# Linear attention and a two-layer network: decays kept over units of 256 tokens, another division of the weights' decoding, 48-column weight loads, new figures in the scheduler

## The chip, the cores and the metric

The kernel runs on one core of one Trainium2 chip. The metric is the time of one execution on the device in microseconds (us). Engines are called by their names in the profile too: TensorE (PE, and PEld for its weight loads), VectorE (DVE), ScalarE (ACT), GpSimd (POOL), and SP, whose queue issues most DMAs.

## The reference

A gated linear attention over 4 batches, 8 heads, 768 tokens and 48 dimensions a head feeds a network of 384, 2048 and 384 columns, all in fp32:

```python
for t in range(S):
    kt, vt, rt, wt = (k[:, :, t], v[:, :, t], r[:, :, t], w[:, :, t])
    cur = np.einsum('bhd,bhe->bhde', u[None] * kt, vt)
    y[:, :, t] = np.einsum('bhd,bhde->bhe', rt, state + cur)
    state = wt[:, :, :, None] * state + np.einsum('bhd,bhe->bhde', kt, vt)
...
h = x @ w_in                       # x: attention's output, (B * S, 384)
g = np.where(pos, h, np.where(neg, 0.0, (h + beta) ** 2 / (4.0 * beta)))
return (g @ w_out).astype(np.float32)
```

`w` is drawn evenly from 0.8 to 0.95, `r`, `k`, `v` and `u` are normal with a spread of 0.1.

## The kernel before

**Units and chunks.** Attention works in 12 units of 256 tokens (UT), three to a batch, and each unit in four chunks of 64 (C, NC). All eight heads of a unit are held at once as four pairs on two tiles (`q`), each head in 64 partitions (HP) of which 48 (D) carry data.

**Attention of one unit** (`attention`, from L350 on). Two scans on VectorE (L405 forward, L400 backward, both in `scan`) give for each chunk the running product P of the decays and its inverse; the seeds tile restarts the running product in every chunk, and `ptot` keeps each chunk's last P (L425). L428 makes k/P and L478 makes r P, in place. `among` (L448) multiplies both in 64x64 tiles, all against all tokens of a chunk; L454 (`picked`) keeps what lies below the diagonal. In the first four units (EARLY) the diagonal with u is made in the same way from k times u, which `with_u` (L416, GpSimd) computes with one instruction for each half of a tile, with u as a per-partition scalar; later units make it from L466, L468, L471 and L474. `ktrans` (L487) transposes k/P on TensorE, ScalarE copies it (L494), `umat` (L509) multiplies it with v, and `chain` (L525 to L528, VectorE) carries the state from chunk to chunk: add, then multiply by the chunk's P. `cross` and `along` (both L550, through `put` and `inter`) add the states' part and the part within a chunk to y. L602 to L606 split y into a rounded part and a rest for the network; six DMAs a unit (L649, `fill`) spread the fourth pair of heads into the rows that the others leave free.

**The network** (`products`, from L694 on). Blocks of 512 tokens (two units) go through 16 slices of 128 hidden columns. Each slice takes nine matmuls in (L896, `product_in`: high times high, low times high, high times low, for three slices of rows) and nine out (L916, `product_out`), two slices later (LAG). Between them, the gate: L712 and L713 on ScalarE, L714 on VectorE, L716 rounds on ScalarE, L717 gives the rest on VectorE. HALVES splits some slices into two halves of 256 tokens, one unit each: the first 5 of block 0 and the first 11 of block 1. So block 0 can begin with unit 0 alone.

**Weights** (`weight`, from L309 on). They come as 64-bit words. For each of the 16 slices: load (L317), magnitude of the high word (L326, ScalarE), low bits (L329, ScalarE) and sign (L330, GpSimd) into the two halves of one buffer `rr`, both joined with the magnitude (L332, VectorE), the high part rounded (L322, ScalarE), and the low part as a difference (L335, VectorE). There is one `rr`, two `fl`, and three loads may be in flight.

**Order of the work.** Nothing is left to run-time choice. `Plan` records every operation with an engine, a cost in us and what it reads and writes; `port=True` marks those that use the port which VectorE and GpSimd share, and they are never planned at the same time. `order` plays them through with those costs, HOP us from one engine to the next, and picks on each engine the ready one that is due first; `best` repeats this six times (ROUNDS) and keeps the order that ends first. LEADS, DECODE, SLACK, STEP, FIRST and PACED set the dues at the start. `kept_warm` puts matmuls on zeros (L304) into planned gaps of TensorE; `warm` (L298) does the same at the start. The emitted order then holds on each engine, in sequence.

**Guard.** `check` looks at the end whether all P are at least P_MIN and all decays at most 1; if not, `general` computes everything again.

## Time and profile before

| what | value |
|---|---|
| median of 3 runs | 529.23 us (528.53 to 530.14) |
| span of the profiled execution | 526.9 us |
| TensorE busy | 503.0 us (95%), 5438 matmuls |
| its weight loads (PEld) | 412.2 us (78%) |
| VectorE busy | 340.4 us (65%), 592 instructions |
| ScalarE busy | 294.4 us (56%), 596 instructions |
| GpSimd busy | 108.8 us (21%), 76 instructions |
| mean granted clock of TensorE | 0.991 |
| moved by DMA | 54.22 MB |

The span runs from the first to the last instruction of one execution; the runs' times contain a little more around it. In the profile's rows, "xN" is the number of instructions, "busy, mean ns" their time together and the mean of one, and behind the second bar stands the idle time of the engine just ahead of them with what ended most of it. A timeline's row has the start, the length, engine, line, operation, and the idle time before it in brackets. A row of the chain has the start, the length and what it was. Matmuls overlap, so a busy TensorE isn't TensorE at its peak; the step from one group's start to the next group's start is the better measure.

### The profile page before, as it was taken

How to read it: one execution, taken by the hardware profiler on the slowest of the kernel's cores; microseconds unless marked ns; L12 is line 12 of the kernel's file. 1: busy time of each engine (PE TensorE's matmuls, PEld its weight loads, DVE VectorE, ACT ScalarE, POOL GpSimd, SP SyncE). 2: the span in 40 equal slices, each digit the busy share in tenths (PEclk: the TensorE clock that was granted, in tenths of full speed). 3: DMA queues.
4: the chain of work that ended last, by engine and by line, in shares of the span. 5: the costliest groups of instructions: out<-in, count | busy, mean ns of one | idle time of the engine just before them, and what ended most of it. 6: DMA issues, size and time to landing. Idle time of an engine off the chain costs nothing.

```text
span 526.9 us, 12832 instructions
## 1 busy us (share of the span) xinstructions
PE 503.0 (95%) x5438; PEld 412.2 (78%) x5438; DVE 340.4 (65%) x592; ACT 294.4 (56%) x596; POOL 108.8 (21%) x76
## 2 busy tenths in 40 slices
PE   7778899999999999999999999999999999999993
PEld 5557787788999988887877778887787777788882
DVE  5989799999897868324398869445833545333331
ACT  1387698878786556433464736443744444444441
POOL 6496865740203021000111011101000100000000
PEclk9899999999999999999999999999999999999997
DMA  8865472344835171100234404103200100100001
GB/s 321 344 240 179 152 318 81 122 148 145 271 104 181 44 237 48 61 0 3 82 125 140 151 20 151 56 2 109 78 0 2 41 17 12 66 0 1 0 0 67
DMA packets 21921, 54.22 MB, mean 103 GB/s; under 512 B 3104, under 2 KB 8672, under 8 KB 21856
## 3 DMA queue, kind: packets, MB, share of 16 engines
q1 hardware_dynamic: 21568, 52.93, 29.2%
q8 instruction: 44, 0.72, 0.5%
q10 hardware_dynamic: 288, 0.39, 0.2%
q14 instruction: 21, 0.17, 0.1%
HBM read 46.43 MB, written 4.72 MB: 97 GB/s over the span
## 4 chain that ended last, share of the span: by engine, by line
PE 77%; POOL 6%; DVE 5%; issue 4%; DMA 3%; ACT 1%; SPq 1%; ACTq 0%; DVEq 0%; POOLq 0%
PE h L896 35%; PE acc L916 33%; POOL rr L330 4%; PE bank L550 3%; POOL nk L416 3%; PE bank L509 2%; PE bank L448 2%; PE bank L487 1%; DMA rk<-in_rk 1%; DVE fl L332 1%; SPq L649 1%; DMA cst<-in_consts 1%; DVE y L400 1%; DVE p L405 1%; DVE gl L717 1%
## 5 line engine op out<-in xcount | busy, mean ns | idle before, releaser
L896 PE MATMUL h<-x,wt 128*128 128x512 f32 (+1 forms) x1008 | 223.7, 367 | 2.4 <-DVE wt L335 1.5
L896 PEld LDWEIGHTS h<-x,wt 128*128 128x128 f32 x1008 | 169.6, 188 | 36.2 <-DVE wt L335 2.2
L916 PE MATMUL acc<-gh,wt 128*128 128x512 f32 (+1 forms) x672 | 156.4, 368 | 0.0
L714 DVE SCALAR_TENSOR_TENSOR g<-g,h 128x512 f32<-128x512 f32 (+1 forms) x112 | 67.9, 606 | 99.8 <-ACT g L713 97.5
L916 PEld LDWEIGHTS acc<-gh,wt 128*128 128x128 f32 x672 | 114.0, 188 | 22.1 <-issue 0.5
L712 ACT ACTIVATE g<-h 128x512 f32<-128x512 f32 (+1 forms) x112 | 60.0, 536 | 116.6 <-PE h L896 113.4
L717 DVE TENSOR_TENSOR gl<-g,gh 128x512 fp32r<-128x512 f32 (+1 forms) x112 | 71.5, 640 | 35.6 <-ACT gh L716 35.6
L916 PE MATMUL acc<-gl,wt 128*128 128x512 f32 (+1 forms) x336 | 86.1, 364 | 1.1 <-DVE gl L717 1.1
L716 ACT CAST gh<-g 128x512 fp32r<-128x512 f32 (+1 forms) x112 | 62.2, 556 | 44.4 <-DVE g L714 42.1
L916 PEld LDWEIGHTS acc<-gl,wt 128*128 128x128 f32 x336 | 58.7, 188 | 12.5 <-DVE gl L717 1.5
L713 ACT ACTIVATE g<-g 128x512 f32<-128x512 f32 (+1 forms) x112 | 63.9, 571 | 3.2
L474 POOL TENSOR_TENSOR r<-cst,d 128x512 f32<-128x512 f32 x16 | 16.8, 1070 | 227.5 <-PE bank L550 207.9
L330 POOL TENSOR_SCALAR rr<-wraw 128x768 uint16<-128x768 f32 x16 | 51.6, 3227 | 28.4 <-DVE fl L332 25.1
L405 DVE TENSOR_TENSOR_SCAN p<-wq,seeds 128x520 f32<-128x520 f32 x24 | 30.8, 1283 | 3.1 <-DMA wq<-in_w 2.3
L400 DVE TENSOR_TENSOR_SCAN y<-wq,seeds 128x520 f32<-128x520 f32 x24 | 30.4, 1266 | 0.8
L466 POOL TENSOR_TENSOR nk<-nk 128x768 f32<-128x768 f32 x8 | 15.3, 1914 | 52.5 <-DMA nk<-in_nk 52.5
L416 POOL TENSOR_SCALAR nk<-rk,cst 128x256 f32<-128x256 f32 x16 | 22.5, 1417 | 3.4 <-DMA cst<-in_consts 2.6
L428 DVE TENSOR_TENSOR rk<-rk,y 128x512 f32<-128x512 f32 x24 | 17.9, 745 | 3.6 <-POOL nk L416 2.3
L329 ACT ACTIVATE rr<-wraw 128x768 uint16<-128x768 uint32 x16 | 17.4, 1085 | 1.1 <-DMA wraw<-in_wbits 1.1
L550 PEld LDWEIGHTS bank<-rk,st 64*64 64x64 f32 x656 | 12.3, 134 | 6.9 <-issue 3.7
L454 DVE COPY_PREDICATED r<-below,bank 128x512 f32<-128x512 int32 x22 | 15.1, 727 | 4.0 <-PE bank L448 4.0
L478 DVE TENSOR_TENSOR rk<-rk,p 128x512 f32<-128x512 f32 x24 | 17.4, 736 | 0.3 <-PE acc L448 0.3
(104 smaller groups left out, 398.7 us busy)
## 6 DMA issues: line engine op xcount, KB each, us to landing
rk<-in_rk SPq DMA_DIRECT2D x24, 512.0 KB, 4.6
wraw<-in_wbits SPq DMA_DIRECT2D x16, 768.0 KB, 7.1
wq<-in_w SPq DMA_DIRECT2D x24, 260.5 KB, 2.8
nk<-in_nk SPq DMA_DIRECT2D x8, 768.0 KB, 4.6
vn<-in_v SPq DMA_DIRECT2D x11, 384.0 KB, 6.7
fl<-in_w SPq DMA_DIRECT2D x12, 260.0 KB, 3.1
out_y<-g SPq DMA_DIRECT2D x10, 256.0 KB, 2.5
x<-last SPq DMA_DIRECT2D x66, 32.0 KB, 2.9
```

What stands on the lines that cost most here:

```text
L330: op("POOL", 2.0, due, [("raw", f)], ["rr_high"], lambda: G.tensor_scalar(out=r16[:, :, 1], in0=wraw[f][:, :, 1].bitcast(F32), scalar1=0.0 ...
L400: V.tensor_tensor_scan(out=y_[:, ::-1], data0=w[:, SEG:0:-1], data1=sv[:, ::-1], initial=0.0, op0=ALU.mult, op1=ALU.add)
L405: V.tensor_tensor_scan(out=pv[:, q].rearrange("p n c -> p (n c)"), data0=w[:, 0:SEG], data1=sv, initial=0.0, op0=ALU.mult, op1=ALU.add,)
L416: G.tensor_scalar(out=ku[:, q, cs], in0=rk[slot[q]][:, 1, cs], scalar1=u_col[:, 2 * q + pr : 2 * q + pr + 1], scalar2=None, op0=ALU.mult)
L550: PE.matmul(out=bank[by[g]][HP * half : HP * half + HP, lo : lo + C], start=first, stop=False, skip_group_check=True, **kw)
L712: op("ACT", c, due, [("b", 6 + hk)], [("g", gk)], lambda: nc.scalar.activation(gs, hs, AF.Relu, scale=0.5, bias=0.5))
L713: op("ACT", c, due, (), [("g", gk)], lambda: nc.scalar.activation(gs, gs, AF.Square))
L714: op("DVE", 0.13 + 0.53 * k, due, [("b", 6 + hk)], [("g", gk)], lambda: nc.vector.scalar_tensor_tensor(out=gs, in0=gs, scalar=1.0, in1=hs, ...
L716: op("ACT", c, due, [("g", gk)], [("gh", gk)], lambda: nc.scalar.copy(ghs, gs))
L717: op("DVE", 0.15 + 0.5 * k, due, [("g", gk), ("gh", gk)], [("gl", gk)], lambda: nc.vector.tensor_tensor(out=gls, in0=gs, in1=ghs.bitcast(F ...
L896: nc.tensor.matmul(hp, lhsT=wx[f][:, cs], rhs=xt[:, j, :], start=n == 0, stop=n == 8)
L916: nc.tensor.matmul(o[j], lhsT=wx[f][:, cs], rhs=gt, start=first and i == 0, stop=stop and i == 2, skip_group_check=True)
```

## The change

- The running product is kept over the whole unit of 256 tokens instead of each chunk of 64. P_MIN goes from 2^-58 to 2^-64; seeds, `ptot` and the layout of w follow. `chain` now only adds in each chunk; one multiplication by the unit's P (`carry`) at the end of a unit makes the next unit's first state.
- The sign of the weights is masked out with one instruction on VectorE into `rr`, ScalarE then writes the low bits into the lower halves, and the low part (the difference) moves to GpSimd, not marked with `port`.
- k times u is one tensor product a tile on GpSimd, with u broadcast, in place of two instructions with a scalar.
- The weight loads of `umat` take 48 columns of k instead of 64, those of `cross` and `along` 48 columns of state or v (64 still in units 0 and 6, INPLACE), and the states' part contracts over 48 rows instead of 64.
- `warm` writes zeros of 512 columns to all eight banks, in place of eight matmuls of 128 columns to one.
- The scheduler gets new costs, a shorter HOP, a latency with which an engine's next operation may begin before the last one's end, a price for turning between 64x64 tiles and the full array, separate leads for each weight (DECODES), and new dues.

The diff, cut to its core:

```diff
-SEG = 2 * NC * (C + 1)
+SEG = 2 * (UT + 1)
-P_MIN = 2.0**-58
+P_MIN = 2.0**-64
...
-    HOP = 0.15
+    HOP = 0.04
+    LATENCY = {"PE": 0.16, "DVE": 0.083, "ACT": 0.1}
+    TURN = {64: 0.33, 128: 0.10}
+    ISSUE = 0.75
...
-            free[e] = end[n] = t + op["cost"]
+            end[n] = t + op["cost"]
+            if e == "PE" and op["mode"] != mode:
+                mode = op["mode"]
+                end[n] += self.TURN[mode]
+            free[e] = end[n] - late.get(e, 0.0)
...
-SLACK = 1.95
-LEAD, DECODE = 15, 4.5
-STEP, FIRST, PACED = 4.9, 24.0, 4.6
+SLACK = 5.214
+LEAD = 15
+STEP, FIRST, PACED, AFTER = 10.1576, -2.570, 9.5357, 4.9
...
     def warm():
-        for _ in range(WARM):
-            PE.matmul(hp[0][:, 0:128], lhsT=zero, rhs=zero, start=True, stop=True)
+        for b in bank:
+            PE.matmul(b, lhsT=zero, rhs=zero.unsqueeze(1).broadcast_to([128, 4, 128]), start=True, stop=True)
...
-        op("ACT", 1.07, due, [("raw", f), ("flight", f % FLIGHT)], ["rr_low"],
+        op("DVE", 0.5, due, [("raw", f)], ["rr"], lambda: V.tensor_scalar(
+            out=rr, in0=wraw[f][:, :, 1], scalar1=-(2**31), scalar2=None, op0=ALU.bitwise_and))
+        op("ACT", 1.07, due, [("raw", f), ("flight", f % FLIGHT)], ["rr"],
            lambda: A.activation(r16[:, :, 0], wraw[f][:, :, 0].bitcast(U32), AF.Copy, scale=LOW))
-        op("POOL", 2.0, due, [("raw", f)], ["rr_high"], lambda: G.tensor_scalar(
-            out=r16[:, :, 1], in0=wraw[f][:, :, 1].bitcast(F32), scalar1=0.0, scalar2=32768.0, op0=ALU.is_lt, op1=ALU.mult))
-        op("DVE", 0.95, due, ["rr_low", "rr_high"], [("fl", k)], lambda: V.scalar_tensor_tensor(
+        op("DVE", 0.95, due, ["rr"], [("fl", k)], lambda: V.scalar_tensor_tensor(
             out=m, in0=m, scalar=3, in1=rr, op0=ALU.logical_shift_left, op1=ALU.bitwise_or), port=True)
         op("ACT", 0.83, due, [("fl", k)], [("wh", f), ("raw", f)], split)
-        op("DVE", 0.95, due, [("fl", k), ("wh", f)], [("wl", f)], lambda: V.tensor_tensor(
-            out=w_lo[f], in0=s, in1=w_hi[f].bitcast(F32), op=ALU.subtract), port=True)
+        op("POOL", 1.8, due, [("fl", k), ("wh", f)], [("wl", f)], lambda: G.tensor_tensor(
+            out=w_lo[f], in0=s, in1=w_hi[f].bitcast(F32), op=ALU.subtract))
-        plan.group(first, when, DECODE)
+        plan.group(first, when, DECODES[f])
...
         def with_u(q):
-            for pr in range(2):
-                cs = slice(pr * UT, pr * UT + UT)
-                G.tensor_scalar(
-                    out=ku[:, q, cs], in0=rk[slot[q]][:, 1, cs], scalar1=u_col[:, 2 * q + pr : 2 * q + pr + 1],
-                    scalar2=None, op0=ALU.mult)
+            G.tensor_tensor(
+                out=ku[:, q].rearrange("p (n c) -> p n c", c=UT), in0=parts(q, 1),
+                in1=u_col[:, 2 * q : 2 * q + 2].unsqueeze(2).broadcast_to([128, 2, UT]), op=ALU.mult)
...
-                            i, o = slice(HP * g, HP * g + HP), slice(HP * h, HP * h + HP)
+                            i, o = slice(HP * g, HP * g + HP), slice(HP * h, HP * h + D)
...
-            if old is None:
-                V.tensor_tensor(out=out, in0=up, in1=pt, op=ALU.mult)
-                return
-            V.tensor_tensor(out=sm, in0=up, in1=ss_(old), op=ALU.add)
-            V.tensor_tensor(out=out, in0=sm, in1=pt, op=ALU.mult)
+            if old is None:
+                V.tensor_copy(ss_(new), up(c))
+            else:
+                V.tensor_tensor(out=ss_(new), in0=up(c), in1=ss_(old), op=ALU.add)
+        def carry(new):
+            V.tensor_tensor(out=ss_(new), in0=sm, in1=ptot[:, 4 * u : 4 * u + 4].unsqueeze(2).broadcast_to([128, 4, D]), op=ALU.mult)
...
+        wide = HP if u in INPLACE else D
-            PE.matmul(out=bank[by[g]][HP * half : HP * half + HP, lo : lo + C], start=first, stop=False, skip_group_check=True, **kw)
+            PE.matmul(out=bank[by[g]][HP * half : HP * half + wide, lo : lo + C], start=first, stop=False, skip_group_check=True, **kw)
...
-            i = slice(HP * h, HP * h + HP)
-            put(g, pair, h, c2, lhsT=wide_st[s][i, pair * HP : pair * HP + HP] if s in wide_st else st[s][i, pair * D : pair * D + HP],
+            i = slice(HP * h, HP * h + D)
+            put(g, pair, h, c2, lhsT=wide_st[s][i, pair * HP : pair * HP + wide] if s in wide_st else st[s][i, pair * D : pair * D + wide],
...
-                                put(g, pair, h, c2, lhsT=vs(i, c2, 2 * pair + h, HP), rhs=r_[h][i, pair, c2, :])
+                                put(g, pair, h, c2, lhsT=vs(i, c2, 2 * pair + h, wide), rhs=r_[h][i, pair, c2, :])
```

More of the change, by code (lines that the diff above doesn't have):

```diff
@@ L73, in add @@
         self.ops.append(dict(e=engine, cost=cost, emit=emit, due=due, deps=deps, port=port, size=size,
-                             fresh=fresh and engine == "PE", touch={*reads, *writes}))
+                             fresh=fresh and engine == "PE", touch={*reads, *writes}, mode=mode))
         return n
@@ L127, in order @@
                 users[m].append(n)
-        free, end, begin, lands = {}, {}, {}, []
+        free, end, begin, lands = {"SP": self.ISSUE}, {}, {}, []
         port = bus = 0.0
-        open_ = {}
+        mode = 128
+        late = self.LATENCY
+        open_ = {e: [] for e in ("PE", "SP", "ACT", "DVE", "POOL")}
         since = {}
@@ L135, in opened @@
             op = ops[n]
-            since[n] = max((end[m] + (0.0 if ops[m]["e"] == op["e"] and not ops[m]["size"] else self.HOP) for m in op["deps"]), default=0.0)
-            open_.setdefault(op["e"], []).append(n)
+            since[n] = max((end[m] + (-late.get(op["e"], 0.0) if ops[m]["e"] == op["e"] and not ops[m]["size"] else self.HOP)
+                            for m in op["deps"]), default=0.0)
+            open_[op["e"]].append(n)
         def ready(n):
@@ L240, in attention_moe @@
     minus_one = one([128, 1], F32, "minus_one")
-    seeds = one([128, 2 * NC, C + 1], F32, "seeds")
+    seeds = one([128, 2, UT + 1], F32, "seeds")
     zero = one([128, 128], F32, "zero")
     look = one([1, 2], F32, "look")
-    ptot = one([128, 16 * NU], F32, "ptot")
+    ptot = one([128, 4 * NU], F32, "ptot")
     above = one([128, 2 * NU], F32, "above")
@@ L296, in warm @@
     def warm():
[L297 to L300 removed]
+        for b in bank:
+            PE.matmul(b, lhsT=zero, rhs=zero.unsqueeze(1).broadcast_to([128, 4, 128]), start=True, stop=True)
+    op("PE", 5.5, SOON, ["zero"], [("b", i) for i in range(8)], warm)
     def zeros(b, us):
@@ L524, in chain @@
             if old is None:
-                V.tensor_tensor(out=out, in0=up, in1=pt, op=ALU.mult)
-                return
-            V.tensor_tensor(out=sm, in0=up, in1=ss_(old), op=ALU.add)
-            V.tensor_tensor(out=out, in0=sm, in1=pt, op=ALU.mult)
-        for c in range(NC - (third == UB - 1)):
-            old, new = before[-1], (state["st"] + 1) % STATES
-            if alone and c < NC - 1:
+                V.tensor_copy(ss_(new), up(c))
+            else:
+                V.tensor_tensor(out=ss_(new), in0=up(c), in1=ss_(old), op=ALU.add)
@@ L533, in attention @@
+        def carry(new):
+            V.tensor_tensor(out=ss_(new), in0=sm, in1=ptot[:, 4 * u : 4 * u + 4].unsqueeze(2).broadcast_to([128, 4, D]), op=ALU.mult)
+        for c in range(NC - 1):
+            old = before[-1]
+            if alone:
                 new = list(wide_st)[c]
             else:
-                state["st"] = new
-            op("DVE", 0.35 if old is None else 0.71, due, [("b", bu[c % 2]), ("ptot", u, 0), ("ptot", u, 1)] + ([("s", old)] if old is not None else []),
-               [("s", new), "sm"], lambda c=c, old=old, new=new: chain(c, old, new), port=True)
+                new = state["st"] = (state["st"] + 1) % STATES
+            op("DVE", 0.36, due, [("b", bu[c % 2])] + ([("s", old)] if old is not None else []), [("s", new)],
+               lambda c=c, old=old, new=new: chain(c, old, new), port=True)
@@ L538, in attention @@
             before.append(new)
+        if third != UB - 1:
+            old = before[-1]
+            new = state["st"] = (state["st"] + 1) % STATES
+            op("DVE", 0.36, due, [("b", bu[1]), ("s", old)], ["sm"], lambda old=old: V.tensor_tensor(
+                out=sm, in0=up(NC - 1), in1=ss_(old), op=ALU.add), port=True)
+            op("DVE", 0.36, due, ["sm", ("ptot", u, 0), ("ptot", u, 1)], [("s", new)], lambda new=new: carry(new), port=True)
         by = [take(), take()]
         begun = set()
+        wide = HP if u in INPLACE else D
```

78 lines of the change are left out of this document (38 added, 40 removed).

## The prediction, made before the change was run

> **What bounds the kernel now.** I read the table of windows first, with the edges put where TensorE's pattern changes. After each stretch's length stand the busy times of PE, PEld, DVE, ACT and POOL, then the granted clock.
>
> ```profile
> 0.00:28.90 28.90, 22.23 (x362) 15.77 (x363) 21.16 (x34) 10.16 (x21) 17.40 (x29) 0.94 0.90 334
> 28.90:62.70 33.80, 26.49 (x519) 22.79 (x517) 28.66 (x51) 23.93 (x47) 27.30 (x14) 1.00 0.53 195
> 62.70:518.50 455.80, 454.24 (x4559) 373.64 (x4559) 290.18 (x510) 259.63 (x529) 64.14 (x35) 1.00 0.25 81
> ```
>
> From 62.70 to 518.50 TensorE is busy for 454.24 of 455.80 us. No other engine can shorten that stretch: only less TensorE work, or more of it done before 62.70, does. The 8.4 us from there to the end of the span, 526.9, are copies and stores that the change leaves alone. So the next view is the chain that ended last, which steps from group to group there and so gives what each costs from one start to the next.
>
> ```profile
> 72.14 2.10 PE h L896 x9
> 74.24 1.09 PE bank L448 x64
> 75.33 2.31 PE h L896 x9
> ...
> 84.83 1.08 PE bank L509 x64
> ...
> 92.43 0.63 PE bank L550 x32
> 93.05 2.31 PE h L896 x9
> 95.36 1.56 PE bank L550 x96
> ```
>
> Nine products of 512 columns cost 2.10 us, and 0.2 more behind a group of 64x64 tiles. In the tiled groups, L550's 96 instructions less its 32 take 0.93 us: 16 rounds of four (one to each quarter of the array) at 58 ns. L509 streams 48 columns and L448 streams 64, yet 64 instructions take 1.08 and 1.09 us: the streamed columns don't set the round. What did TensorE achieve before 62.70? Its groups in that window say:
>
> ```profile
> L896 PE MATMUL h<-x,wt 128*128 128x256 f32 x72 | 11.0, 292 | 1.6 <-DVE wt L335 1.5
> ```
>
> 72 first products of 256 columns are eight groups of nine at half of 2.1 us, and the second products trail by up to two steps (LAG), so six groups: some 14 x 1.05 = 14.7 us. Attention for units 0 and 1, with 2 x 1.09 for L448, 1.08 for L509, 0.63 + 1.56 for L550 and about 1 for transposes (two at 0.4 to 0.6 by the plan's costs in the diff), is 6.5 us each, with one more L448 group 14 together, and the turns of mode 2. So about 31 us of 62.7 were useful and 32 were idle, filler or slow. This is the second place where time can come from.
>
> Why so late? The first half of block 0 runs only five weights (HALVES); then unit 1 must be ready. The timelines of VectorE, GpSimd, the SP queue and TensorE show its path:
>
> ```profile
> 11.59 0.69 DVE L428 TENSOR_TENSOR rk<-rk,y 128x512 f32<-128x512 f32 x1 [0.76 <-POOL nk L416]
> ...
> 49.05 0.48 DVE L604 TENSOR_TENSOR last<-bank,last 128x128 fp32r<-128x128 f32 x2
> ```
>
> ```profile
> 6.14 5.41 POOL L416 TENSOR_SCALAR nk<-rk,cst 128x256 f32<-128x256 f32 x4 [2.56 <-DMA cst<-in_consts]
> ```
>
> ```profile
> 22.92 0.81 SPq L277 DMA_DIRECT2D rk<-in_rk  x2
> ...
> 49.59 3.94 SPq L649 DMA_DIRECT2D x<-last  x6
> ```
>
> ```profile
> 56.75 2.30 PE L896 MATMUL h<-x,wt 128*128 128x256 f32 x18
> ```
>
> Unit 1's r and k (L277) load only at 22.92, when unit 0 gives the buffer back, and land 4.6 us later:
>
> ```profile
> rk<-in_rk SPq DMA_DIRECT2D x24, 512.0 KB, 4.6
> ```
>
> So at about 27.5; its last VectorE step ends at 49.53, 22 us on. In the window 28.90 to 62.70 VectorE was busy 28.66 of 33.80 us, GpSimd 27.30: decoding weights and unit 1 fight for them. Six fills take 3.94 us of the queue, and unit 1's first products start at 56.75.
>
> **The change, part by part.** *Weights.* Rows of GpSimd's and VectorE's groups:
>
> ```profile
> L330 POOL TENSOR_SCALAR rr<-wraw 128x768 uint16<-128x768 f32 x16 | 51.6, 3227 | 28.4 <-DVE fl L332 25.1 <-DMA wraw<-in_wbits 3.4
> L416 POOL TENSOR_SCALAR nk<-rk,cst 128x256 f32<-128x256 f32 x16 | 22.5, 1417 | 3.4 <-DMA cst<-in_consts 2.6 <-PE bank L448 0.9
> L474 POOL TENSOR_TENSOR r<-cst,d 128x512 f32<-128x512 f32 x16 | 16.8, 1070 | 227.5 <-PE bank L550 207.9 <-DVE g L714 19.6
> L466 POOL TENSOR_TENSOR nk<-nk 128x768 f32<-128x768 f32 x8 | 15.3, 1914 | 52.5 <-DMA nk<-in_nk 52.5
> ```
>
> ```profile
> L332 DVE SCALAR_TENSOR_TENSOR fl<-fl,rr 128x768 int32<-128x768 int32 x16 | 15.5, 971 | 3.2 <-POOL rr L330 3.1
> L335 DVE TENSOR_TENSOR wt<-fl,wt 128x768 fp32r<-128x768 f32 x16 | 15.2, 949 | 1.0 <-ACT wt L322 1.0
> ...
> L528 DVE TENSOR_TENSOR st<-sm,ptot 128x192 f32<-128x192 f32 x38 | 13.9, 366 | 1.4
> ...
> L673 DVE TENSOR_SCALAR ptot<-ptot 128x192 f32<-128x192 f32 x1 | 0.3, 259 | 0.0
> ```
>
> GpSimd loses 3.23 us a weight and gets the subtraction, like L466: 1.91. The ring through the single rr buffer was 3.23 + 0.97 us; it becomes mask, the low bits on ScalarE, and the OR: 0.6 + 1.1 + 0.97, some 2.7 (1.1 is the plan's cost of L329, which stays as it is). VectorE loses 0.95 and gets the mask. No row shows that instruction. L673, the same operation, did 192 elements in 259 ns, where L528's two tensors needed 366: half the cycles per element, so 768 would take about 0.56 (an estimate); a full-rate one like L335 takes 0.95. I take 0.56: 0.39 less a weight, nothing at the other end. The OR (L332) now waits on ScalarE's low bits behind a mask of its own engine; what stands behind it on VectorE, unit 1's multiplies and the gates L714 and L717, waits along. A wait of the whole 1.1 us would cost more than the mask saves.
>
> *k times u.* Two L416 of 1.42 become one tensor product like L474, 1.07, so four at the start drop from 5.41 to 2.1 us. VectorE's L428 waited 0.76 for them in the row at 11.59, and there are two such multiplies a unit. Taken: 1.5 us at unit 0, and about 1.7 a unit for GpSimd after.
>
> *Decay over whole units.* The chain loses its L528 per chunk but for one: two operations fewer in a batch's first unit, three in the others. At 0.37 that is 0.7 to 1.1 us a unit off VectorE. The scans keep their lengths within 6 of 520 elements. The wide seeds and the smaller ptot save nothing that counts. If the new limit of 2^-64 were broken, the general path would run; with decays drawn evenly from 0.8 to 0.95, 256 of them multiply to about 2^-50, with a spread near one bit, so I leave it out.
>
> *Start of unit 1, summed.* Unit 0 ends 2 us sooner (1.5 + 0.7, some of it lost to longer warm-up fills), so the load lands at 25.5. The 22 us after it hold four L335 (-3.8) and four masks (+2.2), three chain steps (-1.1), and some of the 5.1 us in which VectorE idled in that window, of which I count 2 as gone: 22 becomes 17.5, give or take 3. The last VectorE step ends near 43 instead of 49.5, and the products start near 50 instead of 56.75. TensorE's wait for a decoded weight (1.5 us in L896's row above) goes too. That is 8 to 9 us less idle; I take 9. Cover: if VectorE is late again, ScalarE and GpSimd are not the next limit in that window (23.93 and 27.30 of 33.80 busy, GpSimd to be relieved). The fills' 6 us stay.
>
> *48-column loads.* Load rows:
>
> ```profile
> L896 PEld LDWEIGHTS h<-x,wt 128*128 128x128 f32 x1008 | 169.6, 188 | 36.2 <-DVE wt L335 2.2 <-DMA x<-last 1.3 <-issue 0.5
> ...
> L550 PEld LDWEIGHTS bank<-rk,st 64*64 64x64 f32 x656 | 12.3, 134 | 6.9 <-issue 3.7 <-DVE g L714 1.1 <-ACT gh L716 0.7
> L550 PEld LDWEIGHTS bank<-r,vn 64*64 64x64 f32 x704 | 11.8, 134 | 0.0
> L509 PEld LDWEIGHTS bank<-vn,kt 64*64 64x64 f32 x704 | 11.3, 134 | 4.1 <-issue 1.8 <-ACT kt L494 0.9 <-ACT gh L716 0.4
> ```
>
> 64 columns more cost 188 - 134 = 54 ns, 0.84 a column, nearly a whole round of 58. If loads set the round, 16 columns fewer save 13.5 ns of it. Rounds concerned: L509 in all 12 units, 12 x 16 = 192; L550 in the ten units outside INPLACE, (656 + 704 - 112)/4 = 312 (unit 6 keeps its 112). 504 x 13.5 = 6.8 us, all but some 0.2 in the stretch where TensorE is the end of the chain. If instead a fixed cost per instruction sets the round, the gain is 0. I take 6.8, because equal times for 48 and 64 streamed columns point at the load.
>
> The Trainium skill, "TensorE: Matmul & The Clock Gate", section "LDWEIGHTS (loading the stationary operand)", gives a load time of columns over 1.2 GHz; an estimate by it is 13.3 ns a round, 6.7 us, which agrees with the rows. "TensorEngine Tiling (Array Packing)", section "Instruction Overhead", speaks against: about 60 cycles for each matmul, so that narrow ones cost the same; by it the term could be 0.
>
> *Scheduler.* It only reorders. In the packed stretch there are 1.56 us of idle to win or lose; smaller assumed hops (0.04 instead of 0.15) leave less slack in each fixed order. I take 0, with 2 either way.
>
> Sum: 526.9 - 6.8 - 9 = 511.1 us of span. The median of the runs, 529.23, stands 2.3 above the profiled span, so 513.4, rounded to **513**. Its own range is 508 to 518.
>
> **Rivals.** *A, the start is not won.* The collisions of VectorE and GpSimd, or VectorE waiting in its own queue for the low bits, keep unit 1 at 56.75. For it: VectorE is the fuller engine there, and the new GpSimd subtraction isn't marked as using the shared port in the plan. Against: less work on both. Time: 526.9 - 6.8 + 2.3 = 522.4.
>
> *B, narrow loads save nothing.* 526.9 - 9 + 2.3 = 520.2. For: no row shows a 48-column load. Against: 0.84 ns a column.
>
> *C, the shared port turns VectorE into the bound, and the kernel is slower.* A two-input GpSimd operation holds up VectorE's two-input ones:
>
> ```profile
> 302.37 2.95 DVE L717 TENSOR_TENSOR gl<-g,gh 128x512 fp32r<-128x512 f32 x2 [0.53 <-ACT gh L716]
> ```
>
> ```profile
> 302.59 2.18 POOL L466 TENSOR_TENSOR nk<-nk 128x768 f32<-128x768 f32 x1 [16.55 <-DMA nk<-in_nk]
> ```
>
> Two subtractions of 0.69 took 2.95 us beside L466: the second waited 1.6. There will be 16 such operations for weights and 8 for k times u before block 1. Block 1's products began at 124.8, and up to there VectorE was busy for 109.42 us:
>
> ```profile
> 0.00:124.80 124.80, 110.75 (x1590) 89.32 (x1590) 109.42 (x177) 87.83 (x162) 78.63 (x53) 0.99 0.58 207
> ```
>
> After the edits about 91 are needed (an estimate: less 16 x 0.39, less 3.2 of chain, less some 9 done for unit 3, which may wait). With the 7.7 us that it idled before 28.90 it ends at 98.7 + 20 x, where x is the delay that one subtraction causes (eight shorter products count as four). Slower than before needs x above 1.55, for then block 1 starts later than 124.8 by more than the 5 us that narrow loads give after it. At 1.85 it starts at 135.7, 11 late: 526.9 + 11 - 5 + 2.3 = 535. Against: VectorE's 16 L335 beside L330 kept a mean of 949 ns, and L466's eight caused far less than 1.6 each.
>
> The Trainium skill, "SBUF — State Buffer", section "Who interferes with whom", says the pair of ports is an exclusive lock held for the whole instruction. The pair of rows above agrees; L335 beside L330 does not.
>
> *D, more is won.* Unit 1 also gains from decoding ahead of it, is ready at 44, and TensorE packs 12 to 15 us sooner: 505 to 508.
>
> **How the numbers follow.** 0.3% is 1.6 us, about what a measurement of this kernel tells from no change. Chances: forecast 0.52, A 0.16, B 0.12, D 0.12, C 0.06, no effect 0.02. Slower is C, 0.06; same is no effect and 0.02 of A joined with B, 0.04; the rest, 0.90, is faster. The range, 504 to 523, holds the forecast, A, B and D.
>
> **What would show it.** Right: products of unit 1's half start near 50, TensorE has no gaps from there, L509's 64 instructions take 0.87 and L550's 96 take 1.24, L673's kind of mask takes about 0.56. Wrong: VectorE's two-input operations lengthened beside GpSimd's new subtraction, waits of L332 on ScalarE's low bits, gaps of TensorE after 62.7, or L509 still at 1.08.

## The result, and the profile after

The changed kernel takes 545.66 us (median of 4 runs, 544.35 to 547.12), the kernel before beside it 528.98 (528.53 to 530.14): a ratio of 1.030 [1.027, 1.033], so it is slower, by 16 us by the ratio and 17 by the medians. The forecast was 513 us. The profiled execution's span went from 526.9 to 542.6 us.

The table of windows of the kernel after, with the edges of before and one more at 124.80, where block 1's products used to begin (columns as above: PE, PEld, DVE, ACT, POOL, clock):

```profile
0.00:28.90 28.90, 23.51 (x351) 15.55 (x351) 19.48 (x31) 9.61 (x20) 7.58 (x24) 0.88 0.88 329
28.90:62.70 33.80, 24.71 (x499) 22.65 (x499) 32.58 (x47) 19.59 (x42) 15.61 (x9) 0.85 0.43 153
62.70:124.80 62.10, 52.62 (x553) 42.52 (x553) 59.35 (x80) 47.87 (x81) 24.16 (x12) 1.00 0.46 162
62.70:518.50 455.80, 440.71 (x4509) 360.37 (x4509) 284.24 (x474) 256.25 (x525) 57.22 (x36) 1.00 0.26 85
```

VectorE is full from 28.90 on: 32.58 of 33.80 us (28.66 before), then 59.35 of 62.10. In the second of these stretches it was as full before, but with 95 instructions where it now gets through 80:

```profile
62.70:124.80 62.10, 62.04 (x711) 50.76 (x711) 59.59 (x95) 53.75 (x96) 33.93 (x12) 1.00 0.45 156
```

The stretch in which TensorE had idled 1.56 us now holds 15.1 us of idle time, 9.5 of them before 124.80. In the chain that ended last TensorE hardly appears between 62.70 and 149: two longer pieces, 2.1 us together. Its timeline shows the places:

```profile
40.55 1.98 PE L457 MATMUL bank<-rk 64*64 64x64 f32 x64 [5.68 <-DVE rk L487]
...
60.49 1.70 PE L913 MATMUL h<-x,wt 128*128 128x256 f32 x13
...
137.11 1.30 PE L913 MATMUL h<-x,wt 128*128 128x256 f32 x9
```

Unit 1's products (60.49) begin 3.7 us later than before, not 7 sooner, and block 1's (137.11) 12.3 later than the 124.8 of before. What held the tiles at 40.55 up for 5.68 us stands in VectorE's timeline, beside GpSimd's:

```profile
32.16 2.66 DVE L411 TENSOR_TENSOR_SCAN y<-wq,seeds 128x514 f32<-128x514 f32 x1
34.91 1.29 DVE L437 TENSOR_TENSOR rk<-rk,y 128x512 f32<-128x512 f32 x1
36.12 0.95 DVE L343 SCALAR_TENSOR_TENSOR fl<-fl,rr 128x768 int32<-128x768 int32 x1
36.99 0.72 DVE L463 COPY_PREDICATED r<-cst,bank 128x512 f32<-128x512 int32 x1
37.61 2.89 DVE L487 TENSOR_TENSOR rk<-rk,p 128x512 f32<-128x512 f32 x2
...
45.14 0.56 DVE L339 TENSOR_SCALAR rr<-wraw 128x768 int32<-128x768 int32 x1
...
82.15 2.36 DVE L437 TENSOR_TENSOR rk<-rk,y 128x512 f32<-128x512 f32 x1
...
97.67 2.09 DVE L339 TENSOR_SCALAR rr<-wraw 128x768 int32<-128x768 int32 x1
99.69 2.31 DVE L734 TENSOR_TENSOR gl<-g,gh 128x512 fp32r<-128x512 f32 x1
```

```profile
31.68 2.06 POOL L346 TENSOR_TENSOR wt<-fl,wt 128x768 fp32r<-128x768 f32 x1
33.70 1.96 POOL L425 TENSOR_TENSOR nk<-rk,cst 128x512 f32<-128x512 f32 x1
38.01 1.94 POOL L346 TENSOR_TENSOR wt<-fl,wt 128x768 fp32r<-128x768 f32 x1 [2.36 <-ACT wt L333]
...
82.11 1.85 POOL L346 TENSOR_TENSOR wt<-fl,wt 128x768 fp32r<-128x768 f32 x1 [5.43 <-ACT wt L333]
...
97.40 4.05 POOL L346 TENSOR_TENSOR wt<-fl,wt 128x768 fp32r<-128x768 f32 x2 [2.27 <-ACT wt L333]
```

The scan at 32.16 and the second multiply of L487 are held by a subtraction (L346); the multiply at 34.91 by the merged k times u (L425), which also reads two tensors. At 82.11 GpSimd begins a subtraction of 1.85 us; the multiply L437, begun 0.04 us later, takes 2.36 instead of 0.68: its own time behind what is left of the subtraction. At 97.40 two subtractions in a row hold first the mask (L339, 2.09, where it takes 0.56 alone, as at 45.14), then the gate's rest (L734, 2.31). The means by group say how often that happens:

```profile
L411 DVE TENSOR_TENSOR_SCAN y<-wq,seeds 128x514 f32<-128x514 f32 x24 | 34.4, 1433 | 0.8
...
L437 DVE TENSOR_TENSOR rk<-rk,y 128x512 f32<-128x512 f32 x24 | 21.9, 912 | 1.1 <-POOL nk L425 0.9
L487 DVE TENSOR_TENSOR rk<-rk,p 128x512 f32<-128x512 f32 x24 | 18.8, 792 | 0.7 <-PE acc L457 0.4 <-DMA rk<-in_rk 0.3
L343 DVE SCALAR_TENSOR_TENSOR fl<-fl,rr 128x768 int32<-128x768 int32 x16 | 18.0, 1122 | 3.7 <-ACT rr L342 3.5
...
L339 DVE TENSOR_SCALAR rr<-wraw 128x768 int32<-128x768 int32 x16 | 11.8, 740 | 0.3
```

```profile
L346 POOL TENSOR_TENSOR wt<-fl,wt 128x768 fp32r<-128x768 f32 x16 | 32.7, 2048 | 60.1 <-ACT wt L333 51.6 <-DVE st L536 8.5
```

The OR (L343) is the L332 of before: 1122 ns instead of 971, and it waits 3.5 us for ScalarE's low bits. The prediction named that wait as a sign of being wrong, but L332 had waited 3.1 us for GpSimd's sign before, so it says little. The narrow loads, at last, in the chain that ended last:

```profile
187.97 0.87 PE bank L518 x64
...
192.22 0.59 PE bank L567 x32
...
196.20 1.49 PE bank L567 x96
```

`umat` (L518, the L509 of before) takes 0.87 as forecast; `along` (L567, the L550 of before) 1.49 instead of 1.24.

### The profile page after: what moved, and what is told of

The parts are those of the page before. It is cut to its first block, busy times and chain, and to the rows that moved or that the text cites. A ratio compares the mean times of both kernels' runs of the same rounds, so it can differ in the third digit from the quotient of the medians.

```text
span 542.6 us, 12742 instructions
## 1 busy us (share of the span) xinstructions
PE 504.8 (93%) x5424; PEld 410.8 (76%) x5424; DVE 342.2 (63%) x560; ACT 291.6 (54%) x596; POOL 80.4 (15%) x68
## 4 chain that ended last, share of the span: by engine, by line
PE 69%; DVE 17%; DMA 5%; ACT 4%; issue 3%; SPq 0%; ACTq 0%; DVEq 0%; POOL 0%; POOLq 0%
PE acc L933 29%; PE h L913 28%; PE bank L567 3%; DVE y L411 3%; DVE fl L343 3%; DVE gl L734 2%; DMA out_y<-g 2%; PE bank L457 2%; DVE rk L487 2%; PE bank L496 2%; DVE g L731 1%; DVE rr L339 1%; PE bank L518 1%; DVE p L416 1%; DMA fl<-in_w 1%
## 5 line engine op out<-in xcount | busy, mean ns | idle before, releaser
L734 DVE TENSOR_TENSOR gl<-g,gh 128x512 fp32r<-128x512 f32 (+1 forms) x112 | 73.9, 661 | 38.6 <-ACT gh L733 38.5
L346 POOL TENSOR_TENSOR wt<-fl,wt 128x768 fp32r<-128x768 f32 x16 | 32.7, 2048 | 60.1 <-ACT wt L333 51.6
L411 DVE TENSOR_TENSOR_SCAN y<-wq,seeds 128x514 f32<-128x514 f32 x24 | 34.4, 1433 | 0.8
L416 DVE TENSOR_TENSOR_SCAN p<-wq,seeds 128x514 f32<-128x514 f32 x24 | 31.7, 1321 | 3.6 <-POOL st L305 2.1
L437 DVE TENSOR_TENSOR rk<-rk,y 128x512 f32<-128x512 f32 x24 | 21.9, 912 | 1.1 <-POOL nk L425 0.9
L567 PEld LDWEIGHTS bank<-rk,st 48*48 48x48 f32 (+1 forms) x656 | 11.9, 123 | 12.2 <-DVE st L536 4.0
L567 PE MATMUL bank<-rk,st 48*48 48x64 f32 (+1 forms) x656 | 15.2, 225 | 5.7 <-DVE st L536 3.1
L343 DVE SCALAR_TENSOR_TENSOR fl<-fl,rr 128x768 int32<-128x768 int32 x16 | 18.0, 1122 | 3.7 <-ACT rr L342 3.5
L457 PE MATMUL bank<-rk 64*64 64x64 f32 x704 | 13.6, 230 | 6.7 <-DVE rk L487 6.7
L457 PEld LDWEIGHTS bank<-rk 64*64 64x64 f32 x704 | 12.0, 142 | 9.7 <-DVE rk L487 7.2
```

The costliest lines, as they stand in the source:

```text
L343: op("DVE", 0.95, due, ["rr"], [("fl", k)], lambda: V.scalar_tensor_tensor(out=m, in0=m, scalar=3, in1=rr, op0=ALU.logical_shift_left, op1 ...
L411: V.tensor_tensor_scan(out=y_[:, ::-1], data0=w[:, SEG:0:-1], data1=sv[:, ::-1], initial=0.0, op0=ALU.mult, op1=ALU.add)
L416: V.tensor_tensor_scan(out=pv[:, q].rearrange("p n c -> p (n c)"), data0=w[:, 0:SEG], data1=sv, initial=0.0, op0=ALU.mult, op1=ALU.add,)
L457: PE.matmul(bank[to[h]][HP * g : HP * g + C, lo : lo + C], lhsT=left(q)[i, cs], rhs=rk[slot[q]][i, 0, cs], start=True, stop=True,)
L567: PE.matmul(out=bank[by[g]][HP * half : HP * half + wide, lo : lo + C], start=first, stop=False, skip_group_check=True, **kw)
L734: op("DVE", 0.15 + 0.54 * k, due, [("g", gk), ("gh", gk)], [("gl", gk)], lambda: nc.vector.tensor_tensor(out=gls, in0=gs, in1=ghs.bitcast( ...
```

## The experiments

My theory after the result: GpSimd's subtraction of two tensors and VectorE's instructions on two tensors (and the mask) exclude each other, and this costs most of the loss. The first rival: the planner's new order costs it, whatever the engines do to each other. The second: the warm-up over eight banks delays the start. A third stands in the expectations: VectorE waits behind its mask for ScalarE's low bits. Ratios are to the kernel before, run beside each kernel on the same chip.

**Collisions: taken away, and the low part moved back.** In the first kernel only this line changes, and the order is planned anew:

```diff
-        op("POOL", 1.8, due, [("fl", k), ("wh", f)], [("wl", f)], lambda: G.tensor_tensor(
+        op("DVE", 0.95, due, [("fl", k), ("wh", f)], [("wl", f)], lambda: V.tensor_tensor(
```

> The changed kernel with the weights' low part back on VectorE (0.95 us, marked with port), planned anew; all else as changed. Port theory (GpSimd's 16 new two-input subtractions hold up VectorE's two-input operations, which sum to some 20 us of longer VectorE operations before 180 us): the backward scan's mean falls from 1433 to near 1260 ns, k/P's multiply from 912 to near 740, and the time falls from 545.7 to about 535 in spite of 15 us more VectorE work. Plan theory (the new costs, hops and leads make an order that real times don't keep, whatever the body): 543 to 548. Low-bits theory (VectorE waits in its own queue for ScalarE's low bits behind the mask): also 543 or more, as that wait stays.

536.03 us, ratio 1.010 [1.006, 1.013], near the 535 of the port theory; the scan falls to 1282 ns. The second keeps the order of after instruction by instruction; GpSimd keeps its time for each weight and its waits, but reads hardly anything:

```diff
+        def low():
+            for cs in (slice(0, 8), None, None, slice(760, 768)):
+                if cs is None:
+                    G.memset(w_lo[f][:, 8:760].bitcast(F32), 0.0)
+                else:
+                    G.tensor_tensor(out=w_lo[f][:, cs], in0=s[:, cs], in1=w_hi[f][:, cs].bitcast(F32), op=ALU.subtract)
```

> The changed kernel in its very order, but GpSimd writes zeros twice over the low part, between two subtractions of 8 columns at its ends, instead of subtracting all 768: same engine, same place, some 1.6 to 1.8 us, nearly nothing read from SBUF. The low parts of the weights are left out of the result. Port theory: the long VectorE operations go (backward scan 1433 to 1250 ns, the OR 1122 to 960, the second gate 661 to 645), TensorE's 14 us of gaps between 62.7 and 180 fall to 6 or less, time 530 to 538. Plan theory and low-bits theory: 543 to 546, VectorE's means shorter but the gaps as before.

527.36 us, ratio 0.991 [0.987, 0.994]: in the same order 18 us less than after by the medians, 21 by the ratios. Its groups of VectorE and GpSimd:

```profile
L417 DVE TENSOR_TENSOR_SCAN y<-wq,seeds 128x514 f32<-128x514 f32 x24 | 29.5, 1229 | 0.8
L443 DVE TENSOR_TENSOR rk<-rk,y 128x512 f32<-128x512 f32 x24 | 18.0, 750 | 1.2 <-POOL nk L431 0.9
L493 DVE TENSOR_TENSOR rk<-rk,p 128x512 f32<-128x512 f32 x24 | 16.5, 700 | 1.1 <-PE acc L463 0.8 <-DMA rk<-in_rk 0.3
L343 DVE SCALAR_TENSOR_TENSOR fl<-fl,rr 128x768 int32<-128x768 int32 x16 | 15.2, 952 | 4.8 <-ACT rr L342 2.7 <-ACT fl L337 1.8 <-ACT ptot L440 0.4
...
L339 DVE TENSOR_SCALAR rr<-wraw 128x768 int32<-128x768 int32 x16 | 11.2, 700 | 1.4 <-DMA wraw<-in_wbits 1.1
```

```profile
L349 POOL MEMSET wt<- 128x752 f32 x32 | 23.6, 736 | 0.9
...
L351 POOL TENSOR_TENSOR wt<-fl,wt 128x8 fp32r<-128x8 f32 x32 | 15.1, 474 | 44.6 <-ACT wt L333 38.0 <-DVE st L542 6.6
```

GpSimd works 2.42 us a weight here (twice 736 and twice 474 ns), more than the 2.05 of L346, yet these five groups of VectorE take 90.4 us instead of 104.9. So for VectorE's instructions on two tensors it is not GpSimd's time, nor who waits for it, but what it reads while VectorE works. The Trainium skill, "SBUF — State Buffer", section "Who interferes with whom", says the same: VectorE's second input shares a port with GpSimd's reads, not with an instruction of GpSimd that only writes. The trace agrees for the instructions with two inputs (the OR beside zero writes keeps its 0.95 us).

TensorE follows: unit 1's products begin at 56.02 instead of 60.49, block 1's at 123.57 instead of 137.11. L343 still stands idle for 4.8 us, 2.7 of them for the low bits, so that wait isn't the loss.

The mask, with one input, is another matter. Its mean only falls from 740 to 700 ns. In the kernel after, k times u held it twice (1.28 us) and the subtraction once (2.09); with zero writes k times u holds it twice (1.44), and the zero writes once:

```profile
88.40 1.80 POOL L349 MEMSET wt<- 128x752 f32 x2
88.43 1.10 DVE L339 TENSOR_SCALAR rr<-wraw 128x768 int32<-128x768 int32 x1
```

One thing more differs in this run: the low parts are zeros, so TensorE multiplies other numbers. Its granted clock from 62.70 on is 1.00 in both kernels, and from 28.90 to 62.70 it is 0.95 instead of 0.85, which on 25 busy us is worth 3 us at most (an estimate). That can't be the 18.

**Pieces of a quarter.** The subtraction as four instructions of 192 columns, in the order of after:

```diff
+            for c in range(0, 768, 192):
+                G.tensor_tensor(out=w_lo[f][:, c : c + 192], in0=s[:, c : c + 192], in1=w_hi[f][:, c : c + 192].bitcast(F32), op=ALU.subtract)
```

> The kernel after in its very order, with the subtraction of the low part on GpSimd cut into four instructions of 192 columns each. Main theory (a two-input instruction of GpSimd and a two-input instruction of VectorE exclude each other for the whole length of the one that began): a VectorE instruction that meets a low part now waits for at most one quarter, some 0.5 us instead of up to 1.85 us, so most of the 18 us that the collisions cost come back: 530 to 536 us beside 545.7, backward scans' mean near 1.30 instead of 1.43, mask near 0.6. Rival (the two engines share the port's rate for as long as both are at it, whatever the instruction's length): nothing changes, 544 to 547, or more by the four instructions' fixed costs.

542.73 us, ratio 1.020 [1.017, 1.023]: a third of the loss back by the ratios, not the 530 to 536 us that were expected. One row each of its VectorE, GpSimd and ScalarE groups:

```profile
L414 DVE TENSOR_TENSOR_SCAN y<-wq,seeds 128x514 f32<-128x514 f32 x24 | 30.8, 1285 | 0.8
```

```profile
L348 POOL TENSOR_TENSOR wt<-fl,wt 128x192 fp32r<-128x192 f32 x64 | 54.8, 888 | 43.1 <-ACT wt L333 37.6 <-DVE st L539 5.5
```

```profile
L337 ACT ACTIVATE fl<-wraw 128x768 f32<-128x768 f32 x16 | 14.5, 914 | 14.4 <-POOL wt L348 14.4
```

The step about VectorE was right: the scan falls to 1285 ns, as expected (the mask, expected near 0.6 us, stays at 720 ns). But now GpSimd waits between its pieces: 3.4 us a weight instead of 2.05. So the next weight's magnitude (L337) waits 14.4 us for the `fl` buffer, and all that stands behind it on ScalarE with it. What VectorE no longer waits, GpSimd and ScalarE wait instead.

**The planner.** First the new body under the planner of before (`Plan`'s figures and the constants from SLACK to PACED back as in the diff of the change), then the body of before under the new planner (those hunks alone):

> All changes of the computation (decoding, whole-unit decays, k times u, 48-column loads, warm-up) with the scheduler, costs, leads and dues of before. Plan theory: 515 to 522, the gains of the body without the new plan's losses. Port theory: the collisions stay, so above 533. Low-bits theory: above 533.

> The kernel before with only the scheduler's new figures (hop, latencies, turns, issue, costs, leads for each weight, dues). Plan theory: most of the loss, 540 or more against 529. Port theory and low-bits theory: within 4 us of 529, either way.

534.42 us, ratio 1.007 [1.005, 1.010], and 556.28 us, 1.046 [1.040, 1.052]. So the new order costs 11 us with the new body and 26 with the old. Does it cost that without collisions too? The old planner's order, with the zero writes of above in place of the subtraction:

> The kernel old_plan (the whole body of after under the planner figures of before, 534.4 us) in its very order, with the low parts' subtractions on GpSimd replaced by two writes of zeros between two 8-column subtractions, so the low parts are left out. Theory A (the collisions cost what they cost, order aside): 534.4 less some 15 to 18, so 516 to 520. Theory B (the two losses overlap: the old order leaves gaps in which the subtractions meet less, and the new order is bad only because it counts on subtractions that take nothing from VectorE): 525 to 528, about as the new order without collisions (527.4).

525.57 us, ratio 0.988 [0.985, 0.991]. Theory B held: the old order without collisions is hardly better than the new one without (0.991). Collisions cost 0.020 of before's time in the old order and 0.039 in the new; the five groups of VectorE are 7.4 us longer by them in the old order (99.8 against 92.4) and 14.5 in the new. For the body as changed the new order is thus bad mainly by what it puts side by side. Why it puts more side by side stays open: both planners count on a subtraction of 1.8 us that takes nothing from VectorE. And with the low part on VectorE under the old planner:

> All changes of the computation with the scheduler of before, but the weights' low part on VectorE. Port theory: 12 to 18 us less collisions than in the run of the new body with the old plan (534.4) for 15 us more VectorE work before block 1, which TensorE hides in part: 520 to 528. Low-bits theory (VectorE waits for ScalarE behind its mask): no better than 534.

528.72 us, ratio 0.997 [0.995, 0.999]: a body without the subtraction on GpSimd gains 0.3%. The ratios so far, crosswise:

| body; where the low part is made | planner of before | new planner |
|---|---|---|
| before; VectorE | 1 | 1.046 |
| after; GpSimd | 1.007 | 1.030 |
| after; VectorE | 0.997 | 1.010 |
| after; zero writes on GpSimd | 0.988 | 0.991 |

Only in the last row does the order hardly count. With the low part on VectorE the new order costs 0.013 without any such subtraction on GpSimd, and 0.046 with the body of before, in whose trace the scan keeps its 1266 ns. So the new order also loses time by something that isn't these collisions, and these runs don't show what. Two more took the planner of after apart: the engine figures of before under the new dues (first hunk), and the dues of before, with its LEADS too, under the new figures (second); a third changed one due by a trifle (last):

```diff
-    HOP = 0.04
-    LATENCY = {"PE": 0.16, "DVE": 0.083, "ACT": 0.1}
-    TURN = {64: 0.33, 128: 0.10}
-    ISSUE = 0.75
+    HOP = 0.15
+    LATENCY = {}
+    TURN = {64: 0.0, 128: 0.0}
+    ISSUE = 0.0
...
-SLACK = 5.214
-STEP, FIRST, PACED, AFTER = 10.1576, -2.570, 9.5357, 4.9
+SLACK = 1.95
+DECODES = [4.5] * 16
+STEP, FIRST, PACED, AFTER = 4.9, 24.0, 4.6, 4.9
...
-SLACK = 5.214
+SLACK = 5.2
```

> The kernel after with the due times of the new planner, but its engine figures as before (hop 0.15, no latency, no turn, no issue cost). Theory of figures (they make the bad order): about 535. Theory of due times: 545 or more. Theory that figures and due times belong together and any other pair is worse: over 550, as with new figures and old due times (555.9).

> The kernel after with its new engine figures and costs in the planner, but the due times of before (slack, leads of the units, decode lead, step times). Theory of the due times (the new leads and step times put the second half of unit 1 and block 1 late): about 535, as with the whole planner of before (534.4), and block 1 near 130. Rival (the new engine figures, hop, latency and turn, make the bad order): about 545 as the kernel after, block 1 near 137. In between: both count.

> The kernel after with one due-time factor moved by a trifle, 5.214 to 5.2. It measures how far the planner's order, and with it the time, scatters on its own. If the 11 us of the planner are a property of its figures: 544 to 548. If they are scatter of the search: anywhere from 535 to 556.

543.05 us, ratio 1.023 [1.020, 1.026]; 555.9 us, 1.044 [1.041, 1.047]; 546.23 us, 1.030 [1.026, 1.033]. This trifle doesn't move the time. With the dues of before the new figures are worse still; with the engine figures of before the new dues are a little better than after (1.023 against 1.030). Each half alone loses time against the 1.007 of the old planner.

**Can a planner avoid the collisions?** Flags for the subtraction and k times u, then for the mask as well, then all three under the planner of before:

```diff
-            out=w_lo[f], in0=s, in1=w_hi[f].bitcast(F32), op=ALU.subtract))
+            out=w_lo[f], in0=s, in1=w_hi[f].bitcast(F32), op=ALU.subtract), port=True)
...
-                op("POOL", 1.15, due, [("k", s), "cst"], [("ku", q), "nk"], lambda q=q: with_u(q))
+                op("POOL", 1.15, due, [("k", s), "cst"], [("ku", q), "nk"], lambda q=q: with_u(q), port=True)
...
-            out=rr, in0=wraw[f][:, :, 1], scalar1=-(2**31), scalar2=None, op0=ALU.bitwise_and))
+            out=rr, in0=wraw[f][:, :, 1], scalar1=-(2**31), scalar2=None, op0=ALU.bitwise_and), port=True)
```

> The changed kernel with GpSimd's subtraction and its k times u marked as port users, planned anew. Port theory: the plan then keeps most collisions apart, so that VectorE's backward scans, k/P multiply and OR come near their lone lengths (1240, 684, 950 ns) and the time falls to 530 to 538; if the plan's times drift too far from the chip's for the mark to help, the means stay above 1350, 850 and 1050 and the time at 540 or more.

> The kernel after with the subtraction, the k*u product and the mask all marked as users of the shared port, so that the planner never puts one of GpSimd's beside one of VectorE's. Theory of the planner (the collisions are a fault of the order only): they are gone from the trace, mask near 0.56, backward scan near 1.23, and the time comes down towards 527 to 532. Theory of the port (GpSimd's 24 us and VectorE's 59 us in the 62 us from 62.7 to 124.8 don't fit side by side if they exclude each other, so planning them apart costs what the collisions cost): the stretched means fall, the waits grow, 540 to 545.

> The same three flags under the planner of before (534.4 without them; 528.7 with the low part on VectorE; 525.6 without collisions). Theory of the planner: 526 to 530, so that the low part on GpSimd pays after all, against the 528.7 with it on VectorE. Theory of the port: 532 to 537, no gain from the flags.

543.04 us, ratio 1.023 [1.020, 1.026]; 540.1 us, 1.018 [1.015, 1.021]; 534.74 us, 1.008 [1.005, 1.011], against 1.007 without the flags. With two flags the mask took the collisions:

```profile
L339 DVE TENSOR_SCALAR rr<-wraw 128x768 int32<-128x768 int32 x16 | 15.8, 990 | 0.3
```

With three the mask is rid of most, and from 62.70 to 124.80 VectorE is busy for 52.61 us instead of 59.35:

```profile
L339 DVE TENSOR_SCALAR rr<-wraw 128x768 int32<-128x768 int32 x16 | 9.9, 618 | 0.2
```

```profile
62.70:124.80 62.10, 59.61 (x602) 49.06 (x595) 52.61 (x76) 48.26 (x84) 22.95 (x12) 0.98 0.37 135
```

The scan's mean is still 1370 ns (1229 with zero writes), and the five groups take 95.8 us, between 90.4 and 104.9: on the chip the plan keeps only part of them apart. And the work is still late: GpSimd's 22.95 us and VectorE's 52.61 are 75.6 in 62.1. Not all of them use the port, so this is a hint and no proof; that the flags bring nothing under the old planner is shown.

**The parts that stay.** The narrow loads alone, with the warm-up that they came with:

> The kernel before, its scheduler and its costs, with only the 48-column loads and the warm-up over all eight banks that they need. Load theory (the columns loaded set the round): L509's 64 instructions 0.87, L550's 64 with v 0.87 and its 32 with states 0.47, 6.8 us off, 522. Streaming theory (a round lasts for the longer of load and 64 streamed fp32 columns, so that only L509, which streams 48, gets shorter; the changed kernel's trace shows 0.87 there, but 1.00 for v's 64 and 0.48 and 0.59 for the states' 32): 12 x 0.22 and 10 x 0.1, 3.6 us off, 525 to 526. A longer warm-up takes up to 1 us back in both.

530.5 us, ratio 0.999 [0.997, 1.001], no gain where both theories had one. Then with the decays over whole units and the merged k times u, all under the decoding and the planner of before:

> The kernel before with all of the change but the weights' decoding and the scheduler's figures: whole-unit decays, k times u as one product, 48-column loads, warm-up. Port theory: without GpSimd's new subtraction no losses, 3.6 us from TensorE and 2 to 6 from an earlier start: 519 to 525. If instead some of these parts (the 8 products of k and u use the same port) costs as much as the subtraction: 530 or more.

528.41 us, ratio 0.996 [0.994, 0.998], short of the expected 519 to 525. With the narrow loads alone the start gives back what the rounds gain; unit 1's products begin at

```profile
61.26 1.92 PE L894 MATMUL h<-x,wt 128*128 128x256 f32 x15
```

instead of 56.75. That the warm-up does it was argued, so the next two take the warm-up in one pass, on the kernel just named and on the one with the low part on VectorE:

```diff
-            PE.matmul(b, lhsT=zero, rhs=zero.unsqueeze(1).broadcast_to([128, 4, 128]), start=True, stop=True)
+            PE.matmul(b, lhsT=zero.bitcast(F32R), rhs=zero.bitcast(F32R).unsqueeze(1).broadcast_to([128, 4, 128]), start=True, stop=True)
```

> The kernel before with decays over whole units, k*u in one product and 48-column loads (528.4 before this change), with the warm-up over all eight banks in one-pass F32R instead of fp32. Theory (the warm-up of 9.5 us pushes the first half's work back by some 2 to 4 us, and that eats the narrow loads' gain): the first products begin some 2 us sooner, 525 to 527, ratio to before 0.988 to 0.993. Rival (the start is set by VectorE, the warm-up is hidden): 528 to 529, ratio 0.995 to 0.998. Second rival (less TensorE work at the start lowers the granted clock there): 529 or more.

> The whole change with the planner of before and the low part on VectorE (528.7 before this change), with the same one-pass warm-up. Theory of the warm-up: 525 to 527. Theory of VectorE (28.9 to 62.7 us is full with VectorE work in this body, 33.2 of 33.8 us): no change, 528 to 529. Sum rule: if this and the previous kernel both gain the same, the warm-up is a cost of its own, whatever decodes the weights.

528.96 us, ratio 0.996 [0.993, 0.999], and 529.84 us, 0.997 [0.995, 1.000]: no change. The first window of the one with four passes, and of the one with one:

```profile
0.00:28.90 28.90, 24.22 (x356) 15.31 (x357) 21.37 (x33) 10.62 (x22) 13.63 (x26) 0.94 0.95 351
```

```profile
0.00:28.90 28.90, 19.73 (x344) 15.64 (x345) 20.34 (x31) 9.29 (x21) 14.38 (x26) 0.82 0.92 341
...
8.93 1.11 PE L483 MATMUL bank<-cst,rk 128*128 128x128 f32 x4 [2.87 <-DVE rk L424]
```

The first transposes now come at 8.93 us, but four take 1.11 us, and the granted clock falls from 0.94 to 0.82, as the second rival of the expectation had it. The time is that of the first (528 to 529, the warm-up hidden behind VectorE). Which of the two holds isn't separated; that the longer warm-up costs time is not confirmed, and why the narrow loads alone start late stays open. Last, the first of these two with k times u again in two products:

```diff
-            G.tensor_tensor(
-                out=ku[:, q].rearrange("p (n c) -> p n c", c=UT), in0=parts(q, 1),
-                in1=u_col[:, 2 * q : 2 * q + 2].unsqueeze(2).broadcast_to([128, 2, UT]), op=ALU.mult)
+            for pr in range(2):
+                cs = slice(pr * UT, pr * UT + UT)
+                G.tensor_scalar(
+                    out=ku[:, q, cs], in0=rk[slot[q]][:, 1, cs], scalar1=u_col[:, 2 * q + pr : 2 * q + pr + 1],
+                    scalar2=None, op0=ALU.mult)
```

> The kernel with decays over whole units, k*u merged, 48-column loads and the one-pass warm-up under the planner of before (528.96, ratio 0.9961), with k*u again as two products with a per-row factor. Theory (the merged product reads two tensors and so holds VectorE's products up by 0.8 to 1.4 us each in four or five places): 526 to 528. Rival (it is hidden, or the two instructions cost GpSimd as much): 528 to 530, no difference.

528.1 us, ratio 0.994 [0.992, 0.996]. Its interval overlaps that of the kernel with the merged product, so what the merging costs stays open. It has the lowest ratio of the kernels that leave nothing out, within their noise: decays over whole units, narrow loads and the one-pass warm-up, under the decoding and the planner of before, 0.6% below the kernel before.

## Why the prediction was wrong

*The bound.* Right for the kernel before. It failed as a bound for the kernel after: VectorE took TensorE's place up to block 1.

*The failed step: the weights, and rival C at 0.06.* I had the mechanism, its one pair of rows and the place, and put it aside with "VectorE's 16 L335 beside L330 kept a mean of 949 ns". But L330 is an instruction with one tensor input, and the mean of L335 says little even of L330: of the 14 L335 that meet an L330, 13 begin at least 1.37 us after it did. VectorE's multiply that began with it was held in the kernel before, too, for 0.7 us (1.39 instead of 0.69):

```profile
31.02 3.11 POOL L330 TENSOR_SCALAR rr<-wraw 128x768 uint16<-128x768 f32 x1
```

```profile
31.07 1.39 DVE L428 TENSOR_TENSOR rk<-rk,y 128x512 f32<-128x512 f32 x1 [0.83 <-POOL nk L416]
```

The new subtraction is of the other kind, that of L466, for which the only pair of rows quoted showed a hold of 1.6 us. The kernel with zero writes shows the price: 18 us in the very same order, against a forecast gain of 0.39 us a weight. The mask too, alone 0.55 us, became a victim (740 ns on average, 2.09 us at 97.67), twice of k times u and once of the subtraction.

*Rival C's threshold.* It asked for 1.55 us of delay for each subtraction. The five groups' 14.5 us over 16 subtractions make 0.9, and the kernel was slower all the same. C counted VectorE's work as one packed sum, and took what follows as untouched. Shown instead: a stretch in one place idles TensorE there at once (32.16 to 40.50 in the timeline, where L411, L437 and L487 take 6.8 us; with zero writes the same ones take 3.6, at 1.23, 0.69 and 1.66).

```profile
31.31 1.23 DVE L417 TENSOR_TENSOR_SCAN y<-wq,seeds 128x514 f32<-128x514 f32 x1
32.63 0.69 DVE L443 TENSOR_TENSOR rk<-rk,y 128x512 f32<-128x512 f32 x1
...
34.74 1.66 DVE L493 TENSOR_TENSOR rk<-rk,p 128x512 f32<-128x512 f32 x2
```

*Start of unit 1 (-9).* Wrong by itself too. With the low part on VectorE under the old planner no subtraction collides, and unit 1's last step on VectorE ends 4.8 us sooner than before; but its products begin only near 55.3, in the middle of the 18 below: the last slice of unit 0's half comes first in TensorE's order, and its low part, which the same engine owes, ends at 54.33.

```profile
44.22 0.48 DVE L608 TENSOR_TENSOR last<-bank,last 128x128 fp32r<-128x128 f32 x2
...
53.38 0.95 DVE L333 TENSOR_TENSOR wt<-fl,wt 128x768 fp32r<-128x768 f32 x1
```

```profile
53.99 2.56 PE L900 MATMUL h<-x,wt 128*128 128x256 f32 x18
```

```profile
28.90:62.70 33.80, 27.42 (x525) 22.75 (x518) 33.22 (x59) 26.40 (x52) 4.73 (x3) 1.00 0.59 208
```

VectorE is busy 33.22 of 33.80 us there: the time that unit 1's path no longer takes is filled by other work at once. With zero writes under the old planner, where the low part neither is VectorE's work nor collides, unit 1's products begin near 54.7, again behind the last slice of unit 0's half, which waits for its low part (its last 7 matmuls begin at 53.78). That is 2 us sooner than before, not 7.

*48-column loads (-6.8).* The mechanism was half right, the size off. `umat` saved 0.21 in 12 units, 2.5 us: its rounds now load 48 columns and stream 48. `cross` and `along` saved 0.04 + 0.07 in ten units, 1.1 us: they load 48, but stream 64. Before, 64 loaded with 48 streamed took as long as 64 with 64. Per round that is 13 ns saved where 48 are streamed, and 3.4 where 64 are. By these numbers both ends set the round, the longer one deciding; I had read the equal times as the load's alone. 3.6 us of 6.8.

*Scheduler (0, with 2 either way).* Wrong: 11 us here. "It only reorders" is true, but an order decides what runs side by side: collisions cost 0.039 in the new order and 0.020 in the old.

*k times u and the decays.* Together with the narrow loads and the warm-up they bring 0.4% under the old planner, and the decays, loads and warm-up without the merging 0.6%; no run separates the decays. The merged product took 1471 ns in the kernel after, where the prediction had 1070, and 1143 with zero writes.

*Left open.* Why the new order is so bad under the old body (556.28) wasn't followed up. Neither was a third `fl` buffer beside the quarter pieces tried.

## What to carry to other kernels

Before moving an elementwise operation from VectorE to GpSimd, count the tensors that both engines read: where each read two here, the move didn't relieve VectorE, it stopped it, and the profile's means of the neighbours show it. A rival for which the trace has one clear pair of rows shouldn't be dismissed with an instruction of another kind, nor with a group's mean: look up when the two began. A planner's part is measured by exchanging planner and body crosswise; completing its list of what can't run together brought 0.7 to 1.2% under one planner here and nothing under the other.

## What the runs showed of the hardware that I had not expected

- Zero writes by GpSimd (736 ns each) left VectorE's scan at 1229 ns; subtractions brought it to 1433. The mask, one input and one output, is held as well: 0.55 us alone, 2.09 beside a subtraction, and 1.10 beside zero writes, which don't hold VectorE's instructions on two tensors.
- GpSimd's instruction with one input (L330, 3.1 us) held VectorE's multiply that began 0.05 us after it for 0.7 us. L335, begun 1.37 us or more after an L330, kept 0.93 to 0.96.
- Cutting a GpSimd instruction into quarters shortens VectorE's hold (scan 1433 to 1285 ns), but makes GpSimd itself take longer: 3.4 us a weight instead of 2.05.
- Rounds of 64x64 tiles: with 64 columns loaded, 64 instructions take 1.08 us with 48 streamed and 1.09 with 64; with 48 of both 0.87. Where 64 are streamed, loading 48 saved 0.11 us in 128 instructions.
- A shorter warm-up lowered the granted clock of the first 28.9 us from 0.94 to 0.82 and won nothing.
